# Loading and turning the first q and k in 1 KB packets, with a new table of nudges

## The chip, the cores and the metric

The kernel runs on one core of one Trainium2 chip. The metric is device time in microseconds for one execution of the whole program. The kernel before takes 602.29 us, the median of three runs (601.71 to 604.09). One more execution was profiled; all rows of the trace come from it.

## The reference

Four batches of causal attention with 8 heads of 64 over 768 tokens, where a query sees the 96 latest keys and the first 8 ("global") ones, with an ALiBi bias; then the attention's output, 3072 tokens of 512, goes through two dense layers with a sigmoid gate between them.

```
scores = matmul(q, k.T) / sqrt(D)
rel = pos[:, None] - pos[None, :]
is_global = pos[None, :] < n_global          # 8
is_local = (rel >= 0) & (rel < n_local)      # 96
dist = where(is_global & ~is_local, n_local, abs(rel))
scores = scores - slopes[:, None, None] * dist
scores = where(is_global | is_local, scores, -1e9)
a = softmax(scores)
x = matmul(a, v)  -> 3072 x 512
h = x @ w_in                                 # 512 x 2048
out = (h * sigmoid(1.702 * h)) @ w_out       # 2048 x 512
```

q, k, v are float32, the two weight matrices arrive as float64, and the two counts as int64 scalars.

## The kernel before, in words

**Tiles.** The 3072 tokens are 24 blocks of 128, two blocks make a chunk of 256, and d_ff is cut into 8 steps of 256. The first block of each batch (blocks 0 to 3, the constants EARLY and FIRST) is done in float32, the other 20 in float16 parts, a large one and the small remainder, so that a product is two or three float16 products. Weights come as pairs of 32-bit words; VectorE and ScalarE put each step's 1 MB together into large and small float16 parts, with six operations (`weights`, loads at L206).

**The first four blocks** (`prep_first` and what follows). q and k of a block are loaded as [128 tokens, 8 heads, 64] (L397, one transfer of 256 KB each, runs of 64 floats). A turn (L422) brings them to [64 x 2 heads, 128 tokens] in one PSUM tile `tq` by four float32 transposes of 128x128, two heads each. `taken` (L429) copies the turned q in two halves into `QZ`, whose other halves are zero (so that a product over 128 rows sees one head), and the turned k into `KF`; either ScalarE or VectorE does a copy. Then: scores `s` by float32 products with a bias added by a product (L604, L605), their row maxima `top`, turned to `aux` (L612) and copied to `mT`; scores with the keys on the partitions, `sT` (L623 and the lines behind it); exponents to `pt`; values `pv` (L631), with the last head in `aux`; division to `x`; a turn of x (L689); ScalarE's copy of its large part and VectorE's small part (L693) to `xT`. The PSUM tiles `tq`, `tx` of most blocks, the spares below and the up products `h` share two buffers; scores, values and `sT` have their own.

**The bias.** `places`, `distances`, `counts`, `own`, `other` and `slopes` build, at the start, three 128x128 masks (the block before, two of the own block) and from them `mm`, 8 heads of each. `counts` (L308 to L311) turns the two 64-bit counts, which two small transfers have put on all 128 partitions, into floats `cnt`. The first four blocks need only the last mask (`M1`, L338 on ScalarE); the other blocks need the two others (`M2`, L340, eight operations of 128x256 on VectorE).

**The other blocks and the dense layers.** A later block's probabilities are turned by DMA transposes `pt` (L558) and used by L567 to L569. Chunks 0 to 2 go up by `up` (L787: per step and half, 12 products of 256 columns, x's large part, x's small, and weight's small part with x's large) and all chunks go down by `pile` (L895); chunks 3 to 11 go up by a scheme of seven products (L827). A second reading of inputs, named `again`, and sums over it feed a flag at the end, by which a general version is run if the inputs leave the ranges assumed.

**The order.** Nothing is left to a scheduler. Each piece is a `Task` with a guessed cost on one or more engines, predecessors and buffers; `Work.order` walks through time, gives each free engine the ready task with the earliest due time, and writes down the fixed order of each engine. Due times come from behind, plus what the table `NUDGE` has for the task's tag ("down12" is the down step 2 of chunk 1, "T0" a preparation of weights). Where TensorE has nothing ready, in the first 50 us of the planner's time (WARM), the planner puts in a spare (L1060): two products of 128x512 on constants, planned at their length, or at twice that for the first five.

All loads and DMA transposes go through SyncE's queue in that written order.

Of the kernel before, what the change touches and what calls it, by code (L numbers as in the profile page):

```python
# [19 lines left out]
P = 128  # L20
# [9 lines left out]
NUDGE = {"T2": -1.5, "down02": 1.4, "down05": -8.2, "down07": -0.8, "down103": 6.7, "down113": -5.5,  # L30
# [9 lines left out]
FIRST = 4  # L40
SIGN = [{"DVE": 0.62, "ACT": 1.0}]
TURN_X = 4
WARM, GAP = 50.0, 0.5
# [44 lines left out]
class Work:  # L88
# [15 lines left out]
    def order(self):  # L104
# [18 lines left out]
        for t in self.tasks:  # L123
            t.due += NUDGE.get(t.tag, 0.0)
        free = dict.fromkeys(("PE", "DVE", "ACT", "POOL", "SP"), 0.0)
# [4 lines left out]
        while len(done) < len(self.tasks) + spared:  # L130
            moved = False
            for e in free:
# [21 lines left out]
                if best is None:  # L154
                    if e != "PE" or now > WARM or now < worked + (GAP if worked > 7.0 else 0.0):
                        continue
                    best = self.spare(spared)
                    b = best.bufs[0]
                    if len(b.ring.taken) >= b.ring.bufs and (b.ring.taken[-b.ring.bufs].left or b.ring.taken[-b.ring.bufs].end > now):
                        continue  # L160
                    b.users, b.left = [best], 1
                    ready[best] = now
                    spared += 1
                t, us = best, best.on[e]
# [45 lines left out]
def kernel(  # L210
# [34 lines left out]
    cf = const.tile([P, 2, 2], F32, name="cf")  # L245
# [61 lines left out]
    def counts(e):  # L307
        nc.vector.tensor_copy(cf, ci)  # L308
        nc.vector.tensor_scalar(cnt, cf[:, :, 0], 0.0, None, ALU.is_lt)
        nc.vector.tensor_add(cnt, cnt, cf[:, :, 1])  # L310
        nc.vector.scalar_tensor_tensor(cnt, cnt, float(2 ** 32), cf[:, :, 0], ALU.mult, ALU.add)  # L311
# [29 lines left out]

    wk.tag = "masks"
    m0 = add({"POOL": 2.0}, places, bufs=[ints], want=-9.0)
    m0 = add({"DVE": 1.3}, distances, [m0], [ints, flt, mk], -4.0)
    late = add({"POOL": 1.0}, lambda e: None, [m0], want=0.0)
    m0 = add({"DVE": 0.65}, counts, [m0, late])
    covers = add({"DVE": 1.2}, covered, [m0])
    covers.soon = 300.0
    m1 = add({"DVE": 1.1}, own, [m0], [flt, mk])
# [49 lines left out]

    def guard(n, raw, ld, want):  # L400
# [7 lines left out]
    def prep_first(n):  # L408
# [6 lines left out]
        ld = load(n, raw, (0, 1))  # L415
        turned = []
        for z in range(2):
            tq = Buf(r_h, [P, NU, P], F32, f"tq{n}_{z}")

            def turn(e, z=z, tq=tq):  # L420
                for u in range(NU):
                    nc.tensor.transpose(tq()[:, u], raw()[:, z, 2 * u:2 * u + 2, :].rearrange("p h d -> p (h d)"), ident)  # L422

            turned.append((tq, add({"PE": 4 * TURN}, turn, ld[z:z + 1], [raw, tq])))

        def taken(to, z, part):
            tq, t1 = turned[z]
            return add({"ACT": 0.6, "DVE": 0.7}, lambda e: (
                nc.scalar.mul(to(), tq()[part], SX) if e == "ACT" else nc.vector.tensor_scalar(to(), tq()[part], SX, None, ALU.mult)),  # L429
                [t1], [tq, KF if z else QZ])  # L430

        rows = [slice(D * z, D * z + D) for z in range(2)]
        d["qk_ready"] = [zero, *(taken(lambda z=z: QZ()[rows[z], :, z, :], 0, rows[z]) for z in range(2)), taken(KF, 1, slice(0, P))]
# [85 lines left out]
    def unit(n, u, want_s, want_v):  # L519
# [29 lines left out]
        for j in range(2):  # L549
            t2 = add({"DVE": 0.365}, lambda e, j=j: rows(e, j), [t1, M2], [sp, pr])  # L550
# [30 lines left out]
    def first(n, want):  # L581
# [15 lines left out]
        for f in range(2):  # L597
# [9 lines left out]
            t1 = add({"PE": 4 * (mm_s + MM128)}, scores, [M1[f], *d["qk_ready"]], [sp, *QKs], want + 1.2 * f)  # L607
# [43 lines left out]
    xT, x_ready = {}, {}  # L651

    def finish(n):
# [30 lines left out]
        if n < TURN_X:  # L684
# [7 lines left out]
            t3 = add({"ACT": 0.5}, lambda e: nc.scalar.copy(xT[c]()[:, 0:NCC, t, :], tx()), [t2], [tx, xT[c]])  # L692
            x_ready[n] = add({"DVE": 0.61}, lambda e: nc.vector.tensor_sub(xT[c]()[:, NCC:, t, :], tx(), xT[c]()[:, 0:NCC, t, :]),  # L693
# [84 lines left out]
    def up(c, s, want):  # L778
# [11 lines left out]
        def hh():  # L790
            return ph().rearrange("p f t -> p (f t)")

        t1 = ups[c, s] = [add({"PE": 12 * MM256}, lambda e, fi=fi: mms(e, fi), [x_ready[2 * c], x_ready[2 * c + 1], W_ready[s, 0]],
                  [ph, xT[c], WT[s, 0]], want + 1.3 * fi) for fi in range(2)]
# [262 lines left out]
    def spare(n):  # L1057

        z = Buf(r_h, [P, 4 * P], F32, f"idle{n}")
        return Task({"PE": 2 * MM512 * (2 if n < 5 else 1)}, lambda e: [nc.tensor.matmul(z(), idle[:, 0:P], idle, start=True, stop=True)  # L1060
                                                  for _ in range(2)], (), [z], 0.0)
# [209 lines left out]
```

## Time and profile before

| what | us |
|---|---|
| runs, median (least, most) | 602.29 (601.71, 604.09) |
| the profiled execution | 602.48 |
| its span | 600.7 |
| TensorE busy | 587.5 |
| VectorE busy | 503.0 |
| ScalarE busy | 471.4 |
| GpSimd busy | 5.8 |

The profiled execution's mean granted clock of TensorE is 0.997. A row of the timeline is a start, a length, an engine, a line and operation, the tiles written and read, and in brackets the idle time just before it with what ended it. A DMA queue's row (SPq) runs from issue to landing. Names lose their numbers in the rows, so `tq` is every block's.

### The profile page before, as it was taken

The numbers are of one execution on the slowest core, as the hardware profiler recorded it, in microseconds if no ns is written. First come the engines' busy times: TensorE is split into PE (matmuls) and PEld (weight loads), VectorE is DVE, ScalarE is ACT, GpSimd is POOL, SyncE is SP. The second block draws the span as 40 slices with busy tenths as digits, with TensorE's granted clock in tenths as the row PEclk, the third lists the DMA queues.
The fourth block names the chain that finished last, engine by engine and source line by source line (L and its number), as shares of the span: only waits on it lengthen the run. The fifth ranks groups of instructions, "written<-read, shape, count | busy, mean of one in ns | idle before, by whom it ended". The sixth has DMA issues, their size and how long they took to land.

```text
span 600.7 us, 17037 instructions
## 1 busy us (share of the span) xinstructions
PE 587.5 (98%) x6816; PEld 445.9 (74%) x6816; DVE 503.0 (84%) x1177; ACT 471.4 (78%) x1098; POOL 5.8 (1%) x18
## 2 busy tenths in 40 slices
PE   8989999999999999999999999999999999999996
PEld 5878767777777867777677777777678768867895
DVE  6998999999999999789699789798979978766532
ACT  3878899978768988888698899788999978944432
POOL 3000000000000000000000000000000000000000
PEclk9999999999999999999999999999999999999998
DMA  8998799999976768979996999999989999920001
GB/s 225 310 251 260 227 253 198 191 179 197 212 141 128 156 117 186 196 145 196 216 206 163 226 209 238 197 233 198 236 186 223 224 193 228 234 40 3 36 1 41
DMA packets 268502, 109.58 MB, mean 182 GB/s; under 512 B 249536, under 2 KB 250048, under 8 KB 268416
## 3 DMA queue, kind: packets, MB, share of 16 engines
q1 hardware_dynamic: 267984, 108.30, 86.6%
q8 instruction: 55, 0.90, 0.7%
q14 instruction: 31, 0.25, 0.1%
q10 hardware_dynamic: 432, 0.13, 0.1%
HBM read 57.67 MB, written 6.29 MB: 106 GB/s over the span
## 4 chain that ended last, share of the span: by engine, by line
PE 85%; DMA 7%; ACT 4%; DVE 2%; issue 1%; SPq 1%; POOL 0%; DVEq 0%; ACTq 0%; POOLq 0%
PE y L895 36%; PE pa L827 14%; PE h L787 10%; PE pb L827 10%; PE s L536 5%; DMA pt<-hl 3%; DMA QK<-QK 2%; PE s L604 1%; PE pv L567 1%; PE pv L569 1%; PE pv L568 1%; PE sT L623 1%; PE idle L1060 1%; DMA xT<-x 1%; DMA out_dram<-yo 1%
## 5 line engine op out<-in xcount | busy, mean ns | idle before, releaser
L895 PE MATMUL y<-w,g 128*128 128x512 f16 (+1 forms) x1248 | 266.8, 363 | 0.0
L895 PEld LDWEIGHTS <-g 128*128 128x128 f16 x1248 | 117.9, 98 | 103.3
L827 PEld LDWEIGHTS <-w 128*128 128x128 f16 x1728 | 101.3, 98 | 5.0
L552 ACT ACTIVATE p<-p,NM 128x232 f32<-128x232 f32 x160 | 76.4, 480 | 7.0 <-DVE NM L542 7.0
L827 PEld LDWEIGHTS <-T 128*128 128x128 f16 x1296 | 77.1, 98 | 6.0
L787 PE MATMUL h<-xT,w 128*128 128x256 f16 x576 | 69.4, 273 | 0.3 <-DMA xT<-x 0.2
L542 DVE CUSTOM_DVE_ANT_0 p<-s,mm 128x232 f32<-128x232 f32 x160 | 57.7, 395 | 8.2 <-PE s L536 7.3
L787 PEld LDWEIGHTS <-w 128*128 128x128 f16 x576 | 55.2, 98 | 9.3 <-issue 0.6
L557 DVE TENSOR_TENSOR hl<-p,hl 128x464 f16<-128x464 f32 x80 | 50.9, 636 | 10.2 <-ACT hl L556 10.1
L868 DVE SCALAR_TENSOR_TENSOR g<-t,g 128x512 f16<-128x512 f32 x72 | 49.3, 687 | 11.1 <-ACT g L867 10.9
L867 ACT ACTIVATE g<-t 128x512 f16<-128x512 f32 x72 | 45.0, 628 | 9.5 <-DVE t L860 8.1
L556 ACT CAST hl<-p 128x464 f16<-128x464 f32 x80 | 46.1, 576 | 6.4 <-DMA pt<-hl 4.4
L859 ACT ACTIVATE t<-h 128x512 f32<-128x512 f32 (+1 forms) x72 | 35.9, 515 | 18.2 <-DVE h L835 15.1
L835 DVE TENSOR_TENSOR h<-pb,h 128x256 f32<-128x256 f32 x72 | 29.6, 420 | 23.0 <-PE pb L827 19.6
L827 PE MATMUL pa<-xS,T 128*128 128x128 f16 x648 | 45.0, 219 | 0.0
L860 DVE SCALAR_TENSOR_TENSOR t<-t,h 128x512 f32<-128x512 f32 (+1 forms) x72 | 38.2, 553 | 4.6 <-ACT t L859 4.0
L536 PEld LDWEIGHTS <-QK 128*128 128x128 f16 x640 | 36.5, 98 | 3.7 <-DMA QK<-QK 0.2
L536 PE MATMUL s<-QK 128*128 128x128 f16 x320 | 38.4, 219 | 0.1
L827 PE MATMUL pb<-xS,w 128*128 128x128 f16 x540 | 37.5, 219 | 0.0
L567 PE MATMUL pv<-VR,pt 128*128 128x64 f16 x288 | 34.8, 193 | 2.6 <-DMA pt<-hl 2.6
L827 PE MATMUL pa<-xT,w 128*128 128x128 f16 x540 | 37.0, 219 | 0.0
L569 PE MATMUL pv<-VR,pt 128*128 128x64 f16 x288 | 34.8, 193 | 0.0
(181 smaller groups left out, 1079.9 us busy)
## 6 DMA issues: line engine op xcount, KB each, us to landing
ws<-in_moe_w_in_dram SPq DMA_DIRECT2D x8, 1024.0 KB
ws<-in_moe_w_out_dram SPq DMA_DIRECT2D x8, 1024.0 KB
raw<-in_q_dram SPq DMA_DIRECT2D x24, 256.0 KB
raw<-in_k_dram SPq DMA_DIRECT2D x24, 256.0 KB
out_dram<-yo SPq DMA_DIRECT2D x22, 256.0 KB
QK<-QK SPq DMA_DIRECT2D x40, 128.0 KB
raw<-in_v_dram SPq DMA_DIRECT2D x20, 256.0 KB
ws_00again<-in_moe_w_in_dram SPq DMA_DIRECT2D x8, 512.0 KB
```

The costliest lines, as they stand in the source:

```text
L536: nc.tensor.matmul(sp()[:, j, lo:hi], d["QK"]()[:, 0, h, :], K[:, 1 + z, h, P - (hi - lo):], start=(z == 0), stop=(z == 1), skip_group_che ...
L542: nc.vector.tensor_tensor_reduce(out=pr()[:, j, :], in0=sp()[:, j, :], in1=m, scale=-1.0 / SC, scalar=3.0e38, op0=ALU.add, op1=ALU.min, ac ...
L552: ex.append(add({"ACT": 0.473}, lambda e, j=j: nc.scalar.activation(pr()[:, j, :], pr()[:, j, :], AF.Exp, bias=NM[:, n, hs[j]:hs[j] + 1], ...
L556: t4 = add({"ACT": 0.5}, lambda e: nc.scalar.copy(hl()[:, 0, :, SKIP:], pr()), ex, [pr, hl])
L557: t5 = add({"DVE": 0.55}, lambda e: nc.vector.tensor_sub(hl()[:, 1, :, SKIP:], pr(), hl()[:, 0, :, SKIP:]), [t4], [pr, hl])
L567: nc.tensor.matmul(o, ph, V[:, 0, h], start=(s == 0), stop=False, skip_group_check=True)
L569: nc.tensor.matmul(o, pl, V[:, 0, h], start=False, stop=(s == ns - 1), skip_group_check=True)
L787: nc.tensor.matmul(ph()[:, fi, :], w1(s, cc, z, fi), X[:, y, cc, :], start=(j + cc == 0), stop=(j == 2 and cc == NCC - 1))
L827: nc.tensor.matmul(o()[:, fi], w, x()[:, y * NCC + 2 * k + cc, t], start=(first and fi + j + cc == 0), stop=(last and j + cc == 3), skip_g ...
L867: t4 = add({"ACT": 0.53}, lambda e, g=g, tt=tt: nc.scalar.mul(g()[:, 0], tt(), SG / (SX * SW)), u, [tt, g])
L868: t5 = add({"DVE": 0.61}, lambda e, g=g, tt=tt: nc.vector.scalar_tensor_tensor(g()[:, 1], tt(), SG / (SX * SW), g()[:, 0], ALU.mult, ALU.s ...
L895: nc.tensor.matmul(y(), part(zg, f), w2(s, z, f % 2)[:, m], start=(begin and f + j == 0), stop=(end and j == 2 and f == 2 * len(steps) - 1 ...
```

## The change

1. **Loading.** `load_pairs` replaces `load` for the first four blocks' q and k. Each of q and k is loaded by two transfers of 128 KB, one for the even heads and one for the odd ones. Partition 4j+u holds tokens 4j to 4j+3 of head pair u, which are 1 KB in a row in memory; the 32 groups of tokens j are the outermost index.
2. **Turning.** A turn is now four transposes of 128x64 (even heads, to partitions 0 to 63) and four float32 products with the identity (odd heads, to partitions 64 to 127). The copies `taken` put the tokens back into their order by strided reads of PSUM and strided writes. For blocks 0 and 1 (KHALF = 2) the copy of k is two copies of two head pairs, and each half of the scores waits for its own.
3. **Counts.** The counts are loaded to one partition; a product with a row of ones, `pc`, spreads them, and VectorE copies that to `cnt`.
4. **Wide slopes.** The eight operations of `M2` are given to ScalarE, in four tasks.
5. **First steps' products.** In `up`, for step 0 of chunks 0 and 1, the 16 products with x's large part stand ahead of the 8 with its small part; the 16 no longer wait for the small part.
6. **Spares.** A spare past the fifth is one product, not two. HOLD, a rule of the planner, has an empty table.
7. **NUDGE** has other tags and values, so the written order differs throughout.

```
-NUDGE = {"T2": -1.5, "down02": 1.4, "down05": -8.2, ...}
+NUDGE = {"T0": 4.2, "T1": 0.1, "T3": 0.6, "down01": -3.2, ...}
+KHALF = 2
...
-    ci = const.tile([P, 2, 2], I32, name="ci")
+    ci = const.tile([1, 2, 2], I32, name="ci")
...
-        nc.scalar.dma_start(ci[:, j], src.bitcast(I32).rearrange("(o x) -> o x", o=1).broadcast_to([P, 2]))
+        nc.scalar.dma_start(ci[:, j], src.bitcast(I32).rearrange("(o x) -> o x", o=1))
...
+    m0 = add({"PE": 0.2}, lambda e: nc.tensor.matmul(pc(), row, c1, start=True, stop=True), [m0], [pc], COUNTS)
+    m0 = add({"DVE": 0.15}, lambda e: nc.vector.tensor_copy(cnt, pc()), [m0], [pc], COUNTS)
...
-    M2 = add({"DVE": 2.3, "ACT": 2.6}, lambda e: slopes(e, slice(0, 2)), [m2], [mk])
+    M2 = [add({"ACT": 0.65}, lambda e, f=f: slopes(e, slice(0, 2), range(2 * f, 2 * f + 2)), [m2], [mk]) for f in range(4)]
...
+    def load_pairs(n, raw):
+        b, i = place(n)
+        ld = []
+        for z in range(2):
+            src = (q, k)[z][b, :, i * P:(i + 1) * P, :].rearrange("(u e) (j t) d -> e j u (t d)", e=2, t=4)
+            dst = raw()[:, z].rearrange("p (e t) d -> p e (t d)", e=2)
+            ld.append([add({"SP": 0.45}, lambda e, src=src, dst=dst, o=o: nc.sync.dma_start(dst[:, o], src[o]), bufs=[raw]) for o in range(2)])
+        return ld
...
-                for u in range(NU):
-                    nc.tensor.transpose(tq()[:, u], raw()[:, z, 2 * u:2 * u + 2, :].rearrange("p h d -> p (h d)"), ident)
+                for u in range(4):
+                    nc.tensor.transpose(tq()[0:D, u], raw()[:, z, u, :], ident)
+                for u in range(4):
+                    nc.tensor.matmul(tq()[D:P, u], raw()[:, z, 4 + u, :], ident, start=True, stop=True, skip_group_check=True)
...
+            src = lambda: tq()[part].rearrange("p t (j u) -> p u j t", u=NU)[:, u]
+            dst = lambda: to().rearrange("p u (j t) -> p u j t", t=4)
...
+        if n < KHALF:
+            k_in = [taken(lambda u=u: KF()[:, u:u + 2], 1, slice(0, P), 0.6, slice(u, u + 2)) for u in (0, 2)]
...
+        if s == 0 and c < 2:
+            large = add({"PE": 16 * MM256}, lambda e: [some(e, ((0, 0), (1, 0)), fi, fi == 0, False) for fi in range(2)],
+                        [x_large[2 * c], x_large[2 * c + 1], W_ready[s, 0]], [ph, xT[c], WT[s, 0]], want)
+            t1 = [add({"PE": 8 * MM256}, lambda e: [some(e, ((0, 1),), fi, False, True) for fi in range(2)],
+                      [large, x_ready[2 * c], x_ready[2 * c + 1]], [ph, xT[c], WT[s, 0]], want + 1.8)]
...
-        return Task({"PE": 2 * MM512 * (2 if n < 5 else 1)}, lambda e: [nc.tensor.matmul(z(), idle[:, 0:P], idle, start=True, stop=True)
-                                                  for _ in range(2)], (), [z], 0.0)
+        return Task({"PE": MM512 * (4 if n < 5 else 1)}, lambda e: [nc.tensor.matmul(z(), idle[:, 0:P], idle, start=True, stop=True)
+                                                                    for _ in range(2 if n < 5 else 1)], (), [z], 0.0)
```

**The order at three places.** A row is a line, an operation, the tile written, the tiles read and the shape; `x4` is four in a row (in the rows with brackets the first of four stands alone, and its three likes are left out); weight loads and the second product of a spare are left out; the number behind a name's last underscore is the tile's own, and in `tq0_1` stand block 0 and 1 for k (0 for q). In the new rows the brackets name what the instruction waits for (transfers by their queue, DMAHW; other engines by name).

First the start of TensorE, up to the first score, before:

```order
L1060 MATMUL idle3_137<-idle_71 128x512
L422 MATMUL tq0_0_140<-ident_73,raw0_107 128x128 x4
L1060 MATMUL idle4_146<-idle_71 128x512
L422 MATMUL tq0_1_154<-ident_73,raw0_107 128x128 x4
L1060 MATMUL idle5_168<-idle_71 128x512
L1060 MATMUL idle6_176<-idle_71 128x512
L422 MATMUL tq1_0_182<-ident_73,raw1_115 128x128 x4
L1060 MATMUL idle7_195<-idle_71 128x512
L604 MATMUL s0_0_199<-hl0_89,QZ0_120 128x128
```

and now:

```order
L1112 MATMUL idle3_145<-idle_74 128x512
L449 MATMUL tq0_0_155<-ident_76,raw0_95 64x128 [waits DMAHW1_49,PE_49,Pool_49]
L451 MATMUL tq0_0_155<-ident_76,raw0_95 64x128 [waits DMAHW3_49]
L362 MATMUL pc_168<-c1_68,row_69 128x2 [waits DVE_49]
L449 MATMUL tq0_1_170<-ident_76,raw0_95 64x128 [waits DMAHW4_49,PE_49]
L451 MATMUL tq0_1_170<-ident_76,raw0_95 64x128 [waits DMAHW5_49]
L449 MATMUL tq1_0_190<-ident_76,raw1_96 64x128 [waits DMAHW6_49,PE_49,Activation_49]
L451 MATMUL tq1_0_190<-ident_76,raw1_96 64x128 [waits DMAHW7_49]
L449 MATMUL tq1_1_204<-ident_76,raw1_96 64x128 [waits DMAHW0_49,DVE_49]
L451 MATMUL tq1_1_204<-ident_76,raw1_96 64x128 [waits DMAHW1_49]
L641 MATMUL s0_0_225<-hl0_92,QZ0_142 128x128 [waits Pool_49]
```

Four spares stand ahead of the first turn in both orders (eight products). Behind it, all four turns of blocks 0 and 1 now stand in a row with no spare between them, and the second turn of block 1, which came after scores of block 0, stands ahead of them. The third turn waits for ScalarE: its PSUM buffer is that of the second, which ScalarE's two copies to KF empty.

Then TensorE's end of block 1 and the turns of blocks 2 and 3, before:

```order
L1060 MATMUL idle10_369<-idle_71 128x512
L631 MATMUL pv1_374<-VF1_109,pt1_0_343 128x65 x4
L689 MATMUL tx0_383<-ident_73,x0_365 128x128 x4
L631 MATMUL pv1_374<-VF1_109,pt1_1_381 128x65 x3
L631 MATMUL aux1_304<-VF1_109,pt1_1_381 128x65
L1060 MATMUL idle11_400<-idle_71 128x512
L689 MATMUL tx1_415<-ident_73,x1_408 128x128 x4
L422 MATMUL tq2_0_421<-ident_73,raw2_336 128x128 x4
L422 MATMUL tq2_1_428<-ident_73,raw2_336 128x128 x4
L1060 MATMUL idle12_436<-idle_71 128x512
```

and now:

```order
L449 MATMUL tq2_0_394<-ident_76,raw2_97 64x128 x4
L451 MATMUL tq2_0_394<-ident_76,raw2_97 64x128 x4
L726 MATMUL tx0_406<-ident_76,x0_388 128x128 x4
L668 MATMUL pv1_413<-VF1_115,pt1_0_382 128x65 x4
L668 MATMUL pv1_413<-VF1_115,pt1_1_403 128x65 x3
L668 MATMUL aux1_332<-VF1_115,pt1_1_403 128x65
L449 MATMUL tq2_1_438<-ident_76,raw2_97 64x128 x4
L451 MATMUL tq2_1_438<-ident_76,raw2_97 64x128 x4
L726 MATMUL tx1_449<-ident_76,x1_435 128x128 x4
L449 MATMUL tq3_0_457<-ident_76,raw3_98 64x128 x4
L451 MATMUL tq3_0_457<-ident_76,raw3_98 64x128 x4
```

The spares between these pieces are gone, the first turn of block 2 has moved ahead of block 0's turn of x and block 1's values, and the second follows them. In the whole order 26 spare products are 10: five spares of two, all among the first five.

Last, SyncE's queue at two places of the middle. Around block 13, before:

```order
L700 DMA_TRANSPOSE xT6_4487<-x1612_4426 128x8x128
L206 DMA ws0_10again_4508<-in_moe_w_out_dram 128x1024
L397 DMA raw16_4530<-in_q_dram 128x8x64
L558 DMA_TRANSPOSE pt13_2_4575<-hl0_89 128x8x128
L913 DMA out_0_dram<-yo4_1_4544 128x512
```

and now:

```order
L738 DMA_TRANSPOSE xT6_4532<-x1612_4446 128x8x128
L216 DMA ws0_10again_4538<-in_moe_w_out_dram 128x1024
L965 DMA out_0_dram<-yo4_1_4553 128x512
L595 DMA_TRANSPOSE pt13_2_4602<-hl0_92 128x8x128
L495 DMA_TRANSPOSE QKover14_4644<-qk16over14_1_4297 128x8x128
```

and around block 16, now:

```order
L216 DMA ws2_10again_5818<-in_moe_w_out_dram 128x1024
L414 DMA raw19_5827<-in_q_dram 128x8x64
L595 DMA_TRANSPOSE pt16_1_5870<-hl1_93 128x8x128
```

At block 13 the load of a later block's q that stood between the weight's second reading and the transpose of probabilities has gone elsewhere, and an output store has come in. At block 16 the new order has a re-read and a q load right ahead of such a transpose.

More of the change, by code (lines that the diff above doesn't have):

```diff
@@ L40 @@
 FIRST = 4
+KHALF = 2
 SIGN = [{"DVE": 0.62, "ACT": 1.0}]
 TURN_X = 4
+HOLD = {}
 WARM, GAP = 50.0, 0.5
@@ L124, in order @@
             t.due += NUDGE.get(t.tag, 0.0)
+        held = {}
         free = dict.fromkeys(("PE", "DVE", "ACT", "POOL", "SP"), 0.0)
@@ L163, in order @@
                     spared += 1
+                if e in HOLD and best.due < 1e8:
+                    soon = [at for t, at in ready.items() if e in t.on and now < at <= now + min(HOLD[e], 0.5 * best.on[e]) and
+                            t.due < best.due - 1.0 and t.early() <= at]
+                    if now < held.setdefault((best, e), max(soon, default=0.0)):
+                        continue
                 t, us = best, best.on[e]
@@ L414, in prep_first @@
         zero = add({"POOL": 1.0}, lambda e: [nc.gpsimd.memset(QZ()[D * z:D * z + D, :, 1 - z, :], 0.0) for z in range(2)], bufs=[QZ])
-        ld = load(n, raw, (0, 1))
+        ld = load_pairs(n, raw)
         turned = []
@@ L549, in unit @@
         for j in range(2):
-            t2 = add({"DVE": 0.365}, lambda e, j=j: rows(e, j), [t1, M2], [sp, pr])
+            t2 = add({"DVE": 0.365}, lambda e, j=j: rows(e, j), [t1, *M2], [sp, pr])
             checks.append(t2)
```

52 lines of the change are left out of this document (35 added, 17 removed), and 10 rows, old and new, of the table NUDGE.

## The prediction

> **What bounds the kernel now.** I read the page first, then the windows by stage, the waits of TensorE, and the timeline of the first 40 us.
>
> ```profile
> span 600.7 us, 17037 instructions
> PE 587.5 (98%) x6816; PEld 445.9 (74%) x6816; DVE 503.0 (84%) x1177; ACT 471.4 (78%) x1098; POOL 5.8 (1%) x18
> ...
> 20.00:30.00 10.00, 9.26 (x82) 8.22 (x82) 9.21 (x19) 9.25 (x12) 0.00 (x0) 1.00 1.14 306
> 30.00:40.00 10.00, 7.91 (x67) 6.66 (x67) 9.66 (x14) 7.39 (x11) 0.00 (x0) 1.00 0.81 245
> 580.00:600.70 20.70, 15.37 (x182) 13.81 (x179) 5.10 (x16) 5.25 (x12) 0.00 (x0) 0.93 0.10 30
> ...
> PE pv L567 <- DMA pt<-hl: 2.6, 3, 1.1
> PE idle L1060 <- ACT hl L429: 1.6, 2, 0.9
> PE idle L1060 <- POOL idle L252: 1.3, 1, 1.3
> PE tx L689 <- DVE x L669: 0.7, 1, 0.7
> PE aux L612 <- DVE top L609: 0.6, 1, 0.6
> PE tq L422 <- DVE QZ L429: 0.6, 1, 0.6
> PE h L787 <- DMA xT<-x: 0.2, 1, 0.2
> ```
>
> In the three rows of the windows stand length, busy time of TensorE, its weight loads, VectorE, ScalarE and GpSimd, then the granted clock; the last seven rows are TensorE's waits, as sum, count and longest. TensorE is the bound: busy 98%, and these seven rows hold nearly all that it waits. Only three kinds of time can be won: the first 40 us, 2.8 us of waits in the middle (2.6 for transposed probabilities, 0.2 for x), and the tail. The tail's last output products and the store behind them stand last in the new order too, so its 5.3 us without TensorE stay. From 39.2 us on both kernels owe TensorE the same products.
>
> **The first loads.** They do move faster:
>
> ```profile
> GB/s 0 0 0 0 8 86 193 201 92 106 257 284 248 229 215 201 240 207 234 319 385 397 369 379 312 286 300 361 401 410 414 385 389 377 389 381 328 131 147 270
> ...
> 1.33 3.60 PE L1060 MATMUL idle<-idle 128*128 128x512 bf16 x8 [1.33 <-POOL idle L252]
> 4.75 1.09 PE L422 MATMUL tq<-ident,raw 128*128 128x128 f32 x4
> 5.63 1.06 PE L1060 MATMUL idle<-idle 128*128 128x512 bf16 x2
> 6.83 0.78 PE L422 MATMUL tq<-ident,raw 128*128 128x128 f32 x4
> 8.29 1.02 PE L1060 MATMUL idle<-idle 128*128 128x512 bf16 x4 [0.69 <-ACT hl L429]
> 9.15 0.60 PE L422 MATMUL tq<-ident,raw 128*128 128x128 f32 x4
> 9.58 0.59 PE L1060 MATMUL idle<-idle 128*128 128x512 bf16 x2
> 10.02 0.38 PE L604 MATMUL s<-hl,QZ 128*128 128x128 f32 x2
> ```
>
> The first line has half a microsecond to a slice: 200 to 284 GB/s while q, k and v come in 256-byte runs, 360 to 410 once the weights' rows of 2 and 4 KB take over. The four loads of q and k, 1 MB, need about 4 us at the first rate and 2.7 at the second. But TensorE's order keeps eight spares ahead of the first turn: 1.33 to 4.75, 0.43 each at half clock. The first turn starts at 4.75 today and at 4.75 afterwards, however early q lands. The packets can help only the second to fourth turns (6.83, 9.15, 11.3 now).
>
> **What a turn costs.** Four transposes take 0.43 us (9.15 to 9.58), or 0.88 at half clock (4.75 to 5.63). The new turn has four transposes of the same moving width and four f32 products. A f32 product of 128 columns is two passes:
>
> ```profile
> 10.29 0.44 PE L604 MATMUL s<-hl,QZ 128*128 128x128 f32 x2
> 10.57 0.22 PE L605 MATMUL s<-mm,id 128*128 128x128 bf16 x1
> ...
> L1060 PE MATMUL idle<-idle 128*128 128x512 bf16 x26 | 9.2, 476 | 2.9 <-ACT hl L429 1.6 <-POOL idle L252 1.3
> 32.60 2.78 PE L787 MATMUL h<-xT,w 128*128 128x256 f16 x24
> 35.22 0.39 PE L604 MATMUL s<-hl,QZ 128*128 128x128 f32 x2
> ```
>
> The score product takes 0.28 (10.29 to 10.57) with weight loads of 128 columns; two passes at the rate of a 256-column product are 2 x 0.11 = 0.22 (24 from 32.60 to 35.22). The new products load 64 columns, so I take 0.22; bounds 0.11 (no more than a transpose) and 0.28. The sum up to the first product of the second weight step (39.23 now):
>
> - 8 turns x 4 products x 0.22 = +7.0 us (bounds +3.5 and +9.0);
> - half clock: four products of the first turn cost 0.43, +0.9; the second turn, half of it slow today, comes later and saves 0.3: +0.6;
> - spares: 26 today, 10 in the new order, all of these in the first five tasks: 2 at 0.43 and 14 at 0.22 go, -3.9;
> - waits that the longer turns fill: 1.6 + 0.7 + 0.6 + 0.6 = 3.5 from the rows, five of them counted from a modelled end 0.16 later than the next slot (a transpose's row is 0.27 long, its slot 0.11), +0.8, and two slots of 0.3 ahead of 6.83 and 39.23 that are no wait in the table: -4.9;
> - new waits, +1.5, below.
>
> Together +0.3 us. The cover of the third item is thin: the "single spares" never act, since no spare after the fifth is left in the order.
>
> **The new waits** follow from these copies:
>
> ```profile
> 5.87 0.59 ACT L429 ACTIVATE QZ<-tq 64x512 f32<-64x512 f32 x1 [2.89 <-PE tq L422]
> 6.50 0.69 DVE L429 TENSOR_SCALAR QZ<-tq 64x512 f32<-64x512 f32 x1 [2.57 <-ACT QZ L429]
> 8.02 0.29 DVE L324 TENSOR_SCALAR flt<-flt,cnt 128x128 f32<-128x128 f32 x1
> 9.26 0.91 ACT L338 ACTIVATE mm<-mk 128x128 bf16<-128x128 f32 x4 [1.02 <-DVE mk L327]
> 11.19 1.69 DVE L340 TENSOR_SCALAR mm<-mk 128x256 bf16<-128x256 f32 x8
> 16.21 0.38 PE L623 MATMUL sT<-QZ,hl 128*128 128x128 f32 x2
> 39.23 1.47 PE L787 MATMUL h<-xT,w 128*128 128x256 f16 x12
> ```
>
> First turn: 4.75 + 0.88 + 1.7 = 7.3. ScalarE copies QZ to 8.05, VectorE the other half to 8.8 (it waits for ScalarE, as at 6.50). The second turn ends at 8.7; its PSUM bank is the third's, which waits for both KF halves (two of about 0.32, from 0.91 for four of 128): 9.6, a wait of 0.9. The fourth ends at 12.2, so scores begin at 12.2 instead of 10.02. The masks follow VectorE's QZ and the copied counts: L324's successor at 9.0 instead of 8.02, ready for the products at 11. That is 2.2 us behind; without the interposed spares and the turn inside the scores, the sT products start at 18.0 against 16.21, the last of them end 1.5 late, and the remaining three spares and four waits give that back against four turns of 0.88 more. The second turn of block 2 waits 0.5 for ScalarE's second QZ copy, which stands behind a weight conversion; 0.1 is the counts' small product. The new strided reads of PSUM I take at the old copies' length; no row shows them, and half as long again for the four copies ahead of the scores would be +0.6.
>
> The large-first products move nothing here: x's small half (VectorE, 0.7 after ScalarE's copy) is done within the 16 products x 0.11 that run first. The counts, now read on one partition, were ready before VectorE came to them (it goes from one copy to the next at 6.50 to 8.02), so their shorter transfers win nothing; their new product and copy are the 0.1 above.
>
> One rule speaks against the split turn. The Trainium skill ("TensorEngine Tiling (Array Packing)", Key Properties) says that switching the tiling mode drains TensorE, and a turn is now 128x64 tiles between 128x128 ones. By a drain of 0.16, the part of a row beyond its slot, two switches in each of eight turns would add 2.6 us. The trace already holds such a switch:
>
> ```profile
> 15.61 0.22 PE L605 MATMUL s<-mm,id 128*128 128x128 bf16 x1
> 15.67 0.27 PE L612 MATMUL aux<-ident,top 128*8 128x128 f32 x1
> 15.78 0.59 PE L1060 MATMUL idle<-idle 128*128 128x512 bf16 x2
> ```
>
> The 8-column transpose starts 0.06 after the product before it and the next starts 0.11 later, as everywhere; I see no drain and add nothing.
>
> **The middle.** The table of nudges gives another order. The waits of 2.6 us come where a transpose of probabilities stands behind a weight re-read and a q load in the queue:
>
> ```profile
> 287.56 0.57 SPq L206 DMA_DIRECT2D ws_10again<-in_moe_w_out_dram  x1
> 288.19 0.42 SPq L397 DMA_DIRECT2D raw<-in_q_dram  x1
> 288.71 2.96 SPq L558 DMA_TRANSPOSE pt<-hl  x1
> ...
> 295.25 0.20 PE L567 MATMUL pv<-VR,pt 128*128 128x64 f16 x1 [0.80 <-DMA pt<-hl]
> ```
>
> The new order takes the q load away at this place but makes the same pair at two others (blocks 16 and 22). I expect 2.2 us instead of 2.8; bounds 0 and 5.
>
> So -0.3 us on the profiled execution, whose time is 602.48 (span 600.7 and 1.78 around it): 602.2, and with its 0.2 over the median of the runs, **602.0 us**.
>
> **The rivals.** (a) *Everything is covered*: the new waits don't appear and the middle runs nearly clean, -1.5 and -1.9: 598.6. For it: four short waits in 550 us are all that the middle has now, so a lucky order has none. Against: the third turn's wait for its bank is written in the order, and the pair ahead of a transpose of probabilities stays at two places. 0.20. (b) *The halves of a turn overlap*, since they lie in different columns of the array: 0.43 of each turn hides, 3.4 us, of which the waits on ScalarE take back 0.8: 599.4. It needs an operation that no row of the profile has, two products in different halves of the columns side by side. 0.08. The same page of the Trainium skill says that different tiles run in parallel. (c) *ScalarE becomes the bound of the start*: it gains the eight wide slopes (2.5 us, VectorE's 1.69 before), two QZ copies (1.0) and 0.1 of split copies, 3.6 us; in 20 to 40 us it has 3.4 us free. If its weight conversions and exponents fall behind, TensorE waits at sT, at block 2's turn and at the second weight step, and all 3.6 lands on the path: 605.6. It decides once ScalarE leaves no gap between 16 and 34 us. Against: VectorE sheds 3 us, and with the loads ahead of them shorter the first weights land earlier. 0.12. (d) *The drains are real after all*: 604.6. 0.05.
>
> **The numbers.** The forecast, within 2 us of 602.0 (600.0 to 604.0), has 0.55. About 0.5% (3 us) is what a measurement here can tell from no change. Faster by more: 0.14 of (a), 0.05 of (b), 0.01 of the forecast, 0.20. Slower by more: 0.08 of (c), 0.02 of (d), 0.02 of the forecast, 0.12. The rest, 0.68, is no change. The range from 598.6 to 605.4 leaves out the lower half of (a) and the upper half of (c).
>
> **What would show it.** Right: first turn at 4.75, third turn waiting for ScalarE's copy to about 9.6, scores at about 12.2, the second weight step near 39.5, 64 pass rows of the new products at 0.11, two to four waits for pt of about 1 us. Wrong: scores before 11 or after 13.5; the second weight step before 38 or after 41; turns of 0.9 us (b) or gaps of 0.16 around each (d); ScalarE without a gap and TensorE waiting for it (c).

## The result, and the profile after

The changed kernel takes 605.9 us, the median of ten runs (604.5 to 607.79), beside 601.99 of the kernel before (ten runs, 600.45 to 604.11). The ratio is 1.0063 with a 95% interval of 1.0047 to 1.0079: slower by 0.6%. The forecast was 602.0, no change, and 605.9 lies above its range.

From the page of the changed kernel:

```profile
span 603.4 us, 17163 instructions
PE 593.3 (98%) x6865; PEld 451.2 (75%) x6866; DVE 501.3 (83%) x1171; ACT 473.8 (79%) x1108; POOL 5.8 (1%) x18
```

and its table of TensorE's waits (sum, count, longest):

```profile
PE pa L879 <- ACT h L895: 1.6, 2, 1.3
PE idle L1112 <- POOL idle L265: 1.3, 1, 1.3
PE tq L449 <- ACT hl L460: 0.7, 1, 0.7
PE tq L449 <- ACT QZ L460: 0.5, 1, 0.5
PE pv L604 <- DMA pt<-hl: 0.4, 2, 0.2
```

The profiled execution took 605.54. TensorE waits less than before and is busy 5.8 us longer, so the time did not go into a wait. The timeline of TensorE, from the first turn to the first scores, the first turn of block 2, the second weight step and the last products:

```profile
4.72 1.06 PE L449 MATMUL tq<-ident,raw 128*64 128x128 f32 x4
5.71 1.23 PE L451 MATMUL tq<-ident,raw 128*64 128x128 f32 x8
6.87 0.38 PE L362 MATMUL pc<-c,row 1*128 1x2 f32 x2
7.18 0.62 PE L449 MATMUL tq<-ident,raw 128*64 128x128 f32 x4
7.74 1.09 PE L451 MATMUL tq<-ident,raw 128*64 128x128 f32 x8
9.57 0.63 PE L449 MATMUL tq<-ident,raw 128*64 128x128 f32 x4 [0.75 <-ACT hl L460]
12.72 0.49 PE L641 MATMUL s<-hl,QZ 128*128 128x128 f32 x2
...
26.63 0.22 PE L662 MATMUL sT<-mT,id 128*128 128x128 bf16 x1
26.68 0.60 PE L449 MATMUL tq<-ident,raw 128*64 128x128 f32 x4
27.21 1.09 PE L451 MATMUL tq<-ident,raw 128*64 128x128 f32 x8
28.23 0.66 PE L726 MATMUL tx<-ident,x 128*128 128x128 f32 x4
28.73 0.45 PE L668 MATMUL pv<-VF,pt 128*128 128x65 f32 x3
...
41.91 1.47 PE L825 MATMUL h<-xT,w 128*128 128x256 f16 x12
592.67 5.41 PE L947 MATMUL y<-w,g 128*128 128x256 f16 x48
```

The second weight step starts at 41.91 instead of 39.23, 2.7 us later, and the spans differ by 2.7 too. From there to the last product it is 556.2 us (598.08 less 41.91), and was 556.1 before (595.37 by the row below, less 39.23). So the whole loss of the profiled execution lies in the first 42 us.

```profile
592.58 2.79 PE L895 MATMUL y<-w,g 128*128 128x256 f16 x24
```

A turn's price stands in the block 2 rows. The four transposes take 0.53 (26.68 to 27.21) where four of 128x128 took 0.43; the eight passes of the four products take 1.02 where eight at 0.109 are 0.87; and the four transposes of x behind them take 0.50. In the kernel before, such transposes between products took 0.44:

```profile
25.86 0.61 PE L689 MATMUL tx<-ident,x 128*128 128x128 f32 x4
26.30 0.78 PE L631 MATMUL pv<-VF,pt 128*128 128x65 f32 x6
```

That is 0.30 us more than the 1.31 that the passes alone cost. The 0.05 in the work behind a turn does not show everywhere, so a turn's excess lies between 0.25 and 0.30 us, and eight turns make it 2.0 to 2.4.

### The profile page after: what moved, and what is told of

It reads as the page before. It is cut to its first block, busy times and chain, and to the rows that moved or that the text cites. A ratio compares the mean times of both kernels' runs of the same rounds, so it can differ in the third digit from the quotient of the medians.

```text
span 603.4 us, 17163 instructions
## 1 busy us (share of the span) xinstructions
PE 593.3 (98%) x6865; PEld 451.2 (75%) x6866; DVE 501.3 (83%) x1171; ACT 473.8 (79%) x1108; POOL 5.8 (1%) x18
## 4 chain that ended last, share of the span: by engine, by line
PE 90%; DMA 5%; ACT 2%; DVE 1%; issue 0%; SPq 0%; POOL 0%; DVEq 0%; ACTq 0%; POOLq 0%
PE y L947 39%; PE pa L879 14%; PE pb L879 11%; PE h L825 10%; PE s L573 5%; DMA pt<-hl 2%; PE pv L604 1%; PE s L641 1%; PE pv L606 1%; PE pv L605 1%; PE sT L660 1%; PE tq L451 1%; DMA QK<-qk 1%; DMA ws_11again<-in_moe_w_out_dram 1%; PE h L835 1%; PE pv L668 1%
## 5 line engine op out<-in xcount | busy, mean ns | idle before, releaser
L879 PEld LDWEIGHTS <-w 128*128 128x128 f16 x1728 | 101.8, 98 | 7.2 <-issue 1.6
L825 PE MATMUL h<-xT,w 128*128 128x256 f16 x528 | 63.9, 273 | 0.0
L825 PEld LDWEIGHTS <-w 128*128 128x128 f16 x528 | 50.5, 98 | 7.8
```

What stands on the lines that cost most here:

```text
L825: nc.tensor.matmul(ph()[:, fi, :], w1(s, cc, z, fi), X[:, y, cc, :], start=(j + cc == 0), stop=(j == 2 and cc == NCC - 1))
L879: nc.tensor.matmul(o()[:, fi], w, x()[:, y * NCC + 2 * k + cc, t], start=(first and fi + j + cc == 0), stop=(last and j + cc == 3), skip_g ...
```

## The experiments

All times are medians, and each ratio is to runs of the kernel before that were made alongside. The second weight step's start is from each kernel's timeline (its profiled execution), and differences of half a microsecond in it say little: the first turn starts with passes of double length, which last now longer, now shorter. Two kernels with the same turn, the change and the one with old loads and a split turn, both start it at 4.72; it ends at 6.87 in the one and at 6.38 in the other.

| kernel | a turn, us | second weight step | time, us | ratio to before, 95% |
|---|---|---|---|---|
| before | 0.43 | 39.23 | 601.99 | |
| the change | 1.6 | 41.91 | 605.90 | 1.0047 to 1.0079 |
| old loads, whole transposes | 0.44 | 36.93 | 599.22 | 0.9908 to 0.9956 |
| old loads, whole products | 0.95 | 37.26 | 601.76 | 0.9961 to 0.9997 |
| old loads, split turn | 1.6 | 41.42 | 605.77 | 1.0036 to 1.0073 |
| transpose and product by turns | 2.4 | 47.50 | 612.32 | 1.0131 to 1.0186 |
| eight half products, one half first | 1.6 | 41.28 | 603.96 | 1.0015 to 1.0061 |
| eight half products by turns | 1.15 | 37.60 | 601.49 | 0.9965 to 0.9999 |

**The turn alone, in the changed order.** Three kernels keep every instruction's place of the change and put back the loads of before. One has before's transposes:

```
-        ld = load_pairs(n, raw)
+        ld = [[add({"SP": 0.45}, lambda e, z=z: nc.sync.dma_start(raw()[:, z], (q, k)[z][b, :, i * P:(i + 1) * P, :].rearrange("h p d -> p h d")), bufs=[raw]),
+              add({"SP": 0.45}, lambda e: None, bufs=[raw])] for z in range(2)]
...
-                for u in range(4):
-                    nc.tensor.transpose(tq()[0:D, u], raw()[:, z, u, :], ident)
-                for u in range(4):
-                    nc.tensor.matmul(tq()[D:P, u], raw()[:, z, 4 + u, :], ident, ...)
+                for u in range(NU):
+                    nc.tensor.transpose(tq()[:, u], raw()[:, z, 2 * u:2 * u + 2, :].rearrange("p h d -> p (h d)"), ident)
```

> The changed kernel with the loads and the turns of before (one transfer of 256 KB in runs of 256 bytes, four transposes of 128x128), everything else in the changed order. Theory A (the turn is what costs: 1.6 us in the changed kernel against 0.44): eight turns give back up to 9.3 us of TensorE, of which the waits for loads and copies keep more than half; 601 to 603 us, scores from about 10 us, the second weight step at 38 to 40 us. Theory B (the new order and its copies cost the time, the turns only fill it): 605 to 606, the same second weight step at 41 to 42 with waits ahead of it.

It took 599.22 us (597.71 to 599.64, 7 runs), below what either theory gave, with the second weight step at 36.93, before the 38 of theory A. With old loads and whole transposes the same order is 6.7 us faster than the change, and faster than the kernel before. Theory B, that the order costs the time, is out; that it is the turn and not the loads, the third kernel below shows, which differs from this one in the turn alone.

The next makes the four transposes four products of 128x128 (`nc.tensor.matmul(tq()[:, u], ..., ident)` in place of `nc.tensor.transpose`):

> As the one with the loads and turns of before, but each turn is four f32 products of 128x128 with the identity instead of four transposes: the price of the products without any change of the tile's columns. Theory A: a turn of 0.87 us, 0.44 more, eight of them 3.5 us of TensorE; 1 to 3 us more than with transposes (603 to 605). Theory B: within 1 us of it.

601.76 (600.33 to 603.35, 12 runs), 2.5 us more, the difference that theory A gives (its 603 to 605 stood on a slower kernel with transposes). The second weight step is only 0.33 later, but the two starts are not alike: the first turn began at 4.42 here and at 4.72 there. The profiled execution, of 600.37, also lies 1.4 below the median, so it shows little of the 2.5.

The third has before's loads and the change's split turn:

```
+                for u in range(NU):
+                    nc.tensor.transpose(tq()[0:D, u], raw()[:, z, 2 * u, :], ident)
+                for u in range(NU):
+                    nc.tensor.matmul(tq()[D:P, u], raw()[:, z, 2 * u + 1, :], ident, ...)
```

> The loads of before, with the changed kernel's split turn (four transposes of 64 columns, four products of 64 columns in the other half), in the changed order: only the packets differ from the changed kernel. Theory A: the packets move nothing, since the first turn stands behind the spares and the later ones behind each other; 605 to 607, turns of about 1.6 us. A rival (packets C): q1 and k1 land at about 8 and 9 us and the third and fourth turns or the first weights come later, 1 to 2 us more: 607 to 608.

605.77 (604.0 to 607.95, 12 runs). Beside the kernel with whole transposes, run alongside it, the split turn costs 6.6 us: of the 8.9 us that eight turns take more (1.55 less 0.44 each), about a quarter hides in waits. Beside the change (605.90) it has the old packets and copies without strides, and the two together move nothing that can be measured. The strided copies themselves are as long as the old ones: QZ takes 0.59 us on ScalarE and 0.69 on VectorE in both.

The same place, block 2's turn of q, in the three timelines; whole transposes, whole products, split:

```profile
23.82 0.61 PE L452 MATMUL tq<-ident,raw 128*128 128x128 f32 x4
24.26 0.60 PE L727 MATMUL tx<-ident,x 128*128 128x128 f32 x4
```

```profile
23.37 1.11 PE L452 MATMUL tq<-ident,raw 128*128 128x128 f32 x8
24.32 0.60 PE L728 MATMUL tx<-ident,x 128*128 128x128 f32 x4
```

```profile
26.20 0.60 PE L452 MATMUL tq<-ident,raw 128*64 128x128 f32 x4
26.73 1.09 PE L454 MATMUL tq<-ident,raw 128*64 128x128 f32 x8
27.75 0.66 PE L729 MATMUL tx<-ident,x 128*128 128x128 f32 x4
```

0.44, 0.95 and 1.55 us from the turn's start to the transposes of x. The split turn has twelve passes, four of transposes and eight of products, and these alone would be 1.31.

**More changes of the half.** The change with one transpose and one product by turns:

```
                 for u in range(4):
                     nc.tensor.transpose(tq()[0:D, u], raw()[:, z, u, :], ident)
-                for u in range(4):
                     nc.tensor.matmul(tq()[D:P, u], raw()[:, z, 4 + u, :], ident, ...)
```

> The changed kernel with the four transposes and the four products of a turn in turns (one of each, four times), so that the half of the columns changes eight times a turn and not twice. Theory A (a change of columns makes the next weight load wait for the product before it, about 0.14 us each): six changes more, 0.8 us a turn, eight turns 6.7 us: 611 to 613. A rival (halves run beside each other when a product of the one follows a product of the other): a turn shrinks towards 0.9 us, 602 to 604. A rival (no price for the change; the 0.3 us belong to the first instruction of a new tile or to a wait): 605 to 606.

612.32 (611.82 to 612.82, 6 runs). From its timeline:

```profile
7.19 0.30 PE L449 MATMUL tq<-ident,raw 128*64 128x128 f32 x1
7.42 0.43 PE L450 MATMUL tq<-ident,raw 128*64 128x128 f32 x2
7.78 0.30 PE L449 MATMUL tq<-ident,raw 128*64 128x128 f32 x1
8.01 0.43 PE L450 MATMUL tq<-ident,raw 128*64 128x128 f32 x2
```

A transpose and a product take 0.59 (7.42 to 8.01); three passes at 0.109 are 0.33. Two changes cost 0.26, 0.13 each. A change costs TensorE time, and here the halves do not run beside each other. The time agrees: 6 changes more in each of eight turns are 48, and 6.4 us over the change is 0.13 for each, as theory A expected.

**Columns, or transposes against products?** The change with all eight as half products, four in the lower half of the columns and then four in the upper:

```
-                    nc.tensor.transpose(tq()[0:D, u], raw()[:, z, u, :], ident)
+                    nc.tensor.matmul(tq()[0:D, u], raw()[:, z, u, :], ident, start=True, stop=True, skip_group_check=True)
```

> The changed kernel with the four transposes of a turn made products too: eight products of 64 columns, four in the lower half of the columns and four in the upper, no transpose in the turn. It tells whether the two stalls in a turn belong to the change of columns or to going from transposes to products. Theory A (the columns): the stalls stay at 0.13 to 0.15 us each, a turn is 16 passes of 0.109 and two stalls, 2.0 us, 0.43 more than now; all on the path: 608.5 to 610. Rival (transpose to product): the stall inside the turn goes, a turn of 1.75 to 1.9: 606.5 to 608.

603.96 (602.28 to 608.18, 10 runs): four more passes a turn and no more time, outside both expectations. Theory A in that form fell. Whether the time is less is not shown: the interval overlaps the change's, and the profiled execution took 605.64. The timeline says why the passes cost nothing:

```profile
26.02 0.22 PE L662 MATMUL sT<-mT,id 128*128 128x128 bf16 x1
26.17 0.76 PE L449 MATMUL tq<-ident,raw 128*64 128x128 f32 x5
26.66 0.32 PE L451 MATMUL tq<-ident,raw 128*64 128x128 f32 x1
26.76 0.27 PE L449 MATMUL tq<-ident,raw 128*64 128x128 f32 x1
26.82 0.27 PE L451 MATMUL tq<-ident,raw 128*64 128x128 f32 x1
26.87 0.27 PE L449 MATMUL tq<-ident,raw 128*64 128x128 f32 x1
...
27.04 0.71 PE L451 MATMUL tq<-ident,raw 128*64 128x128 f32 x5
27.68 0.65 PE L726 MATMUL tx<-ident,x 128*128 128x128 f32 x4
```

The upper half's first passes run between the lower half's last ones, two in 0.109 us. Four of a turn's sixteen passes run beside another, so it takes as long as the change's twelve. Between two half products there is no stall, whatever their half. The stalls sit where half products meet anything else: the turn's first product starts at 26.17, 0.15 after the last sT product (26.02, whose slot is 0.055), and the transposes of x start 0.20 after the last pass. A transpose of 64 columns counts as "anything else": in the change it follows the sT product at once (26.63 to 26.68).

The weight loads (PEld) show what stalls. The first row is the transposes of x behind a split turn, in the change, the second those behind whole transposes:

```profile
28.23 0.42 PEld L726 LDWEIGHTS tx<-ident,x 128*128 128x128 f32 x4 [0.17 <-issue]
24.16 0.47 PEld L727 LDWEIGHTS tx<-ident,x 128*128 128x128 f32 x4
```

Behind whole transposes the load starts 0.10 ahead of its first pass (24.26), while the turn still runs; behind the split turn it stands idle for 0.17 and starts together with that pass (28.23).

So the theory became A2: work on a half of the columns and work on the whole array don't overlap, and going from one to the other costs 0.13 to 0.15 us; half products in different halves run side by side. Its test alternates the eight half products:

```
                 for u in range(4):
-                    nc.tensor.transpose(tq()[0:D, u], raw()[:, z, u, :], ident)
-                for u in range(4):
+                    nc.tensor.matmul(tq()[0:D, u], raw()[:, z, u, :], ident, start=True, stop=True, skip_group_check=True)
                     nc.tensor.matmul(tq()[D:P, u], raw()[:, z, 4 + u, :], ident, ...)
```

> The changed kernel, its loads and order, with a turn of eight products of 64 columns (no transposes), one in the lower half of the columns and one in the upper by turns. With all of the lower half first (the kernel of eight products) the last passes of the lower half ran between the first of the upper, and the time was 604.0. Theory A2 (products in different halves run side by side; the stall of 0.13 to 0.15 us belongs to going between whole-array work, transposes of 64 columns among it, and half-array products, once into a turn and once out): 8 passes side by side, 0.87, and two stalls, a turn of 1.15 to 1.25 us against 1.6, eight of them 3 us or more of TensorE: 602 to 604, the second weight step at 38.5 to 40 us. Rival (the old theory A, every change of columns stalls): sixteen passes and eight changes, 2.8 us a turn: 613 to 616.

601.49 (599.99 to 604.5, 12 runs), 4.4 us below the change, and the old theory's 613 is out. Theory A2 has the turn right; the time lies just under its 602 to 604, and the second weight step, 37.60, under its 38.5:

```profile
28.82 0.66 PE L725 MATMUL tx<-ident,x 128*128 128x128 f32 x4
29.41 0.32 PE L449 MATMUL tq<-ident,raw 128*64 128x128 f32 x1
29.41 0.32 PE L450 MATMUL tq<-ident,raw 128*64 128x128 f32 x1
29.57 0.27 PE L449 MATMUL tq<-ident,raw 128*64 128x128 f32 x1
29.57 0.27 PE L450 MATMUL tq<-ident,raw 128*64 128x128 f32 x1
...
30.22 0.27 PE L449 MATMUL tq<-ident,raw 128*64 128x128 f32 x1
30.23 0.27 PE L450 MATMUL tq<-ident,raw 128*64 128x128 f32 x1
30.43 2.79 PE L834 MATMUL h<-xT,w 128*128 128x256 f16 x24
```

Each pass of the lower half has one of the upper beside it. Sixteen passes take eight slots, and the turn 1.1 to 1.2 us with its two stalls.

**The other edits.** The spares of the kernel before, without the last sixteen (`range(2 if n < 5 else 0)`):

> The kernel before without the sixteen spare products after the tenth, all else in its order. The prediction's sum took 3.9 us for them off the path (0.22 each at full clock) and gave most of that back as waits that come to light. Theory A (a spare stands ahead of a wait and costs nothing): within 0.7 us of before, its waits longer by what the spares took. Rival (the spares are on the path): 2 us or more faster.

601.29 (599.57 to 606.78, 12 runs), ratio 0.9976 to 1.0021: no gain that can be told from zero. The waits that the spares covered come to light, 1.3 for x and 1.1 for k's copy among them:

```profile
PE tx L689 <- DVE x L669: 1.3, 1, 1.3
PE s L604 <- ACT hl L429: 1.1, 1, 1.1
PE tq L422 <- DMA raw<-in_k_dram: 1.0, 1, 1.0
```

Two edits undone in the kernel with old loads and whole transposes, order kept. The wide slopes issued on VectorE (`slopes("DVE", ...)`), and the first steps' 24 products in their old order, behind x's small part:

> The changed order with the loads and turns of before, and the eight wide slopes back on VectorE at the same place in the order. Theory A (the time came from the turns, the wide slopes lie beside other work on either engine): within 0.8 us of the same kernel without this edit (599.2). Rival (VectorE's relief is what made this order faster than the kernel before): 601 or more, the first scores' maxima and the sT products later by about 1.5 us.

> The changed order with the loads and turns of before, and the first steps' 24 products in the old order of terms (large, small, weight's small part; one half of d_ff after the other), so that they wait for x's small part. The trace without this edit has 0.38 us of waiting for x's large part ahead of them. Theory A: VectorE's small part comes 0.7 us after ScalarE's large part and after the first four products, so 0.4 to 0.6 us more at chunk 0 and nothing at chunk 1: within 0.8 us (599 to 600). Rival (it is what the new order lives on): 601 or more.

598.53 (597.26 to 599.46, 6 runs; 0.9912 to 0.9957 of before, the lowest median here) and 599.62 (598.85 to 602.27, 12 runs). Undoing either edit moves the time by less than a microsecond. In the first, scores wait 1.8 us for a maximum on VectorE and the second weight step comes at 38.99, two later than with the slopes on ScalarE, yet the whole is no slower; that execution had no wait on TensorE behind it.

Last, the order. The kernel with old loads and turns, their true costs given to the planner, so that it writes another order; the same with the slopes free to go to either engine; and the first with the old table of nudges:

> The changed kernel with the loads and turns of before, and with their true costs given to the planner (1.55 us a load, four transposes a turn), so that the order is written anew; the table of nudges as in the change. In the fixed order VectorE came to the first weights 1.4 to 2.3 us ahead of their transfer and held up the maxima behind them. Theory A (the start then has no such wait): 597 to 599.5, the second weight step at 36 to 37.5 us. Rival (nudges fit one order alone, and another has waits in the middle of 2 us or more): 600 to 602.

> As the order written anew with the true costs, and the planner may give the wide slopes to VectorE or ScalarE (its costs 0.58 and 0.65 us a quarter). Theory A: within 1 us of the former, 597 to 600; the wide slopes are no part of what sets the start. Rival: ScalarE's part in the change is what gains: 600 or more.

> The changed kernel with the loads and turns of before, their true costs in the planner, and the table of nudges of before: what the other edits (counts, half copies of k, wide slopes on ScalarE, large-first products, fewer spares) do with the old table. The same with the new table and an order written anew took 607.5, with the changed order kept 599.2. Theory A (the written order decides, these edits hardly count): a table made for other tasks gives an order of 602 to 608 again. Rival (the edits are worth the 3 us that the kernel with the old turns is faster than before): 598 to 600.

607.49 (603.87 to 608.46, 7 runs), 605.47 (603.0 to 607.79, 12 runs) and 604.61 (601.87 to 607.83, 12 runs). The first differs from the kernel of 599.22 in the written order (with four spares more, and other engines for some copies) and in nothing else. Theory A was wrong for the first two, and the first lies above its rival's 600 to 602 as well. The start was no better, with waits of 1.1 and 1.9 us that the kept order doesn't have:

```profile
PE h L833 <- ACT QZ L458: 1.9, 1, 1.9
PE tx L724 <- DVE x L704: 1.1, 1, 1.1
```

Most of the loss lies behind the start: from the second weight step (37.93) to the end of the span (602.1) this execution takes 564.2 us, the kept order 560.9 (597.8 less 36.93). The third came out in the range of its theory, so the other edits alone, without the order, do not give 599. A table of nudges made for one set of costs did not carry over to another here. What the kept order with whole transposes gained over the kernel before, the split turns lost.

## Why the prediction was wrong

**The step that failed** is the one on the split turn: "I see no drain and add nothing". The two stalls of a turn cost 0.25 to 0.30 us, eight turns 2.0 to 2.4, where the step put nothing. Added to the forecast that gives 604.0 to 604.4, so the stalls are the largest part of the miss of 3.9 us and not all of it. The row that the step leaned on was no witness. It shows a transpose of 8 columns between products of 128; by the change's own row (a 64-column transpose at once behind a product) and by the kernel with eight half products, a transpose of few columns is no work on a part of the array. The trace of before held no half product at all, so it could not speak against the rule, and rival (d), worked out at 604.6, had a chance of 0.05 that should have been far higher. The Trainium skill ("TensorEngine Tiling (Array Packing)", Key Properties) says that changing the tiling mode drains TensorE; the runs agree, at 0.13 to 0.15 us a change, and also with its words that another tile in the same mode is no such change: from half to half nothing stalls.

**Rival (b)** was true of the chip and not of this kernel. Two half products do run side by side, as that section of the Trainium skill says of different tiles, but the change's lower half is made of transposes, and beside those nothing runs. It gave 599.4; the eight half products by turns, which do what it describes, take 601.49, with two stalls left in each turn.

**The passes** were right: 0.109 us each, 64-column products as expected, and the first turn at 4.72 for 4.75. What the forecast calls half clock are passes twice as long (a spare of 0.43 against 0.22); the granted clock of the profile reads 1.00 there. They end earlier than it set: the first turn was over at 6.87, not 7.3. The third turn waited for ScalarE's copy until 9.57 (forecast 9.6), and that match is luck: the time won in the first turn went to the counts' product (6.87 to 7.18, 0.31 for 0.1) and to the second turn's stalls. Scores came at 12.72 for 12.2, by the stalls of the third and fourth turns, which take 1.57 and 1.58 for 1.31. The second turn of block 2 waited 0.52 for ScalarE, as said. The second weight step, 41.91, passed the mark of 41 that was to show the forecast wrong.

**The packets** bring nothing that can be measured, as forecast; the kernel with the old loads shows it (605.77 and 605.90). But that they move faster, as the forecast took from the weights' rates, the trace does not bear out: from 3 to 7 us, by windows of 1 us, the changed kernel moves 172 to 226 GB/s, and the kernel before moved 99 to 270 there; the 360 that the forecast hoped for is not reached.

**The spares and the sum.** The sum had the spares and the filled waits as two terms, -3.9 and -4.9, against 7.0 of longer turns. The kernel before without its last sixteen spares shows that a spare by itself is worth nothing that can be measured, since it stands ahead of a wait. The second weight step came 2.4 later than forecast (41.91 for 39.5), and this equals the stalls' 2.4 by chance, since other terms were off too. By the rows of both timelines the eight turns take about 8.9 us more than before, where the sum had 7.6 (7.0 and 0.6 for the half clock): the stalls added 2.0 to 2.4, and the slow passes, set at 0.6, cost almost nothing more than before. That is 1.3 of the 2.4. The counts' product is 0.2; the other 0.9 is what is left, mostly waits that the longer turns filled less than the sum had.

**The middle.** Expected -0.6. The waits for transposed probabilities did fall, 2.6 to 0.4, and 1.6 on ScalarE's copy of h came in their place; the stretch behind the second weight step is as long as before. In the kernels that keep the changed order this stretch is 553.2 (slopes on VectorE) to 558.2 (eight half products by turns), though the work is nearly the same, so a single profiled execution can't hold a term of 0.6. Of the 3.9 us between the forecast and the time, 2.4 lie ahead of the second weight step and about 0.6 in the middle's gain that did not come. The rest, 0.9, is time outside the profiled spans, which differ by 2.7 where the executions differ by 3.06 (605.54 and 602.48), and what the medians add to that, 3.91 apart. It is not settled further.

**Rivals (c) and (a).** ScalarE did not become the bound: it still has gaps between 16 and 34 us (1.49 us before 20.15), TensorE's table has no wait for its exponents or weights in the start, and slopes on VectorE gain nothing that can be told from zero. Against (a), the new waits for ScalarE's copies are there, 0.7 and 0.5 us.

**Still open:** which edit of the change makes the kept order with whole transposes faster than the kernel before (599.22). Not the slopes and not the large-first products; taking the spares out of the kernel before gained nothing either. The written order is what is left that was seen to move 8 us, but it was not separated from the half copies of k and the counts.

## What to carry to other kernels

Turning a tile with instructions on half of the columns costs more than its passes: count a stall for each meeting of half-array and whole-array work, and if half products are needed, put one of each half by turns so that they run in pairs. A row shows the absence of a cost only if it holds the very operation; where a kernel brings in a kind of instruction that its trace doesn't have, give the rule on it its full weight. Removing spares or shortening transfers that stand ahead of a wait gained nothing here, and a hand-tuned order has to be kept when the part under test is exchanged.

## What the runs showed of the hardware

- Going between half-column products and whole-array work (64-column float32 transposes belong to the latter) stalls TensorE for about 0.13 us where a pass takes 0.109 (two changes in 0.26 us; 48 more changes made the kernel 6.4 us longer).
- Two float32 products in different halves of the columns run side by side when they are issued by turns: sixteen passes in eight slots of 0.109 us. Issued four and four, only about four of the sixteen run beside another.
- A float32 transpose takes one slot of 0.109 us and a float32 product two, with 64 columns as with 128.
